# Attention values as seven block products for eight, placed product by product beside FFN chunks 0 and 1

## The chip, the cores and the metric

One core of a Trainium2 chip. The metric is the device time of the kernel in microseconds (us). The engines that matter here are TensorE (PE; PEld is its weight load, which overlaps the matmuls), VectorE (DVE), ScalarE (ACT), GpSimd (POOL) and SyncE (SP, which only issues DMAs). Each engine runs its own list of instructions strictly in order, so an instruction that waits holds up everything listed behind it on the same engine.

## The reference

A gated mix of two branches over the same 2048 tokens of 512 channels, in float32:

```
q, k, v = split(x @ wqkv)                  # 32 heads of 16 channels
idx  = pos - 2 * arange(8)                 # 8 keys per token, two apart; earlier than 0 is masked
o    = einsum(softmax(q . k[idx] / 4), v[idx])
a    = o @ wo
b    = (gelu(x @ w_gate) * (x @ w_up)) @ w_down      # hidden width 1792
g    = sigmoid((x * gate_w).sum(-1))
out  = g * a + (1 - g) * b
```

## The kernel before

**Parities.** Because the keys lie two tokens apart, even and odd tokens never meet. The kernel handles the even tokens (parity 0) and then the odd ones (parity 1), 1024 tokens each, as two blocks of 512. The first block's x, split by channel halves, is called a11 and a12; the second's a21 and a22. Weights are cut the same way into b11, b12, b21 and b22.

**Split operands.** Every float32 operand is kept as a rounded part ("hi", written by ACT) and the rest ("lo", the raw value minus hi, made by DVE, or by ACT and an adding POOL DMA for the FFN weights). A product of 128-deep operands is three matmuls: hi·hi, lo·hi, hi·lo. A block product over 256 channels is therefore six matmuls.

**Seven for eight.** The gate and up projections of the FFN, and the keys and queries, are made by a seven-product scheme for 2x2 blocks: instead of eight products it uses a11·b11, a12·b21, s1·t1, s2·t2, s3·t3, s4·b22 and a22·t4, where s1 to s4 are sums of token blocks and t1 to t4 sums of weight blocks. The values did not use it: `values(par, jj)` (L174) made, for each of the 8 token tiles jj of a parity, two results of 258 and 256 columns, each from four channel chunks times three matmuls (`qkv_mm`, L124), 192 matmuls a parity. The first result carries two extra columns, of which one is the logit z of the mixing gate.

**Stages.** `start()` (L867) makes keys and queries of parity 0 and prepares the operands of what follows. `ffn(0)` runs 14 FFN chunks; `kq_second()` (L1121) does for parity 1 what `start()` did; `ffn(1)` and an output stage follow. `gate_up` (L521) makes one FFN chunk: seven products into PSUM tiles X_, Z_ and W_ of pool "p" (four banks), with ACT copies (`copy`, L464; the copy of X_ to W_, L539) and DVE adds (`add`, L469) between them; the seventh, a22·t4, is put off into the next chunk (`fourth`). Between its products it calls `idle(i, n)`, which runs side jobs set with `at(i, ...)`, and `piece(i)`. In chunks 0 and 1 the pieces are the value tiles, from chunk 2 on they are the down projection.

**FFN operands.** `operands(par, f, i)` (L403) makes chunk f's weight parts: ACT writes minus the raw value's rounding (L416), a POOL DMA adds the raw value (L417), ACT writes hi (L421). The sums t1 to t4 of the raw weights come from DVE (`combine`, L398; for chunks 0 and 1 of parity 0 `sums`, recorded at L787). A group 0 tile (g with 768 columns hi and 768 lo) holds t1, t2 and b11; group 1 holds the other four.

**Attention.** DVE does nearly all of it: multiplies of 128x2048 (L225, L287) and reductions of the same size (L228), 32 of each kind, with smaller adds. `pull(budget)` advances it by about so many us of work at each call. Its first unit reads the tile kq, whose first rows are filled by a shifted copy (`shift`, L148, two DMAs on ACT's queue for the second half of parity 0).

**Order.** A scheduler places the instructions on the engines by its own estimate of times and by priority; attention has a lower priority than the rest. `Row` (L775) keeps the stages in `start()` and `kq_second()` in the order written, and all that goes through `row`, `act` and `mms` shows under one line, L787. `after` and `ordered` add dependencies by hand.

Of the kernel before, what the change touches and what calls it, by code (L numbers as in the profile page):

```python
# [25 lines left out]
WT = KC * WQ  # L26
WA = 576
DW = 1088
VL = 544
UC = 128  # L30
# [18 lines left out]
def tile_gated_mix(ctx: ExitStack, tc: tile.TileContext, xt, wqkv, wff, wo, out):  # L49
# [5 lines left out]

    BUFS = {"A": 6, "S": 8, "g0": 2, "g1": 2, "d": 4, "raw": 2, "hh": 6, "hl": 6, "c": 4, "s": 3,
            "r": 2, "rt": 4, "p": 4, "lg": 2}

    COLS = {"A": 1024, "S": 1024, "g0": 3 * WA, "g1": 8 * QW, "c": WA, "d": DW, "raw": 8 * QW}

# [62 lines left out]

    def qkv_mm(ps, par, jj, cb, kcs, c0=0, cn=512, behind=None):  # L124
        t = slice((jj % BT) * P, (jj % BT + 1) * P)
        for kc in kcs:
            xh, xl = X[par, jj // BT, kc]
            wh, wl = WC[cb, kc]
            for n, (a, w) in enumerate(((xh, wh), (xl, wh), (xh, wl))):
                LAST[:] = [nc.tensor.matmul(ps[:, :cn], a[:, t], w[:, c0:c0 + cn], start=(kc == 0 and n == 0),  # L130
                                            stop=(kc == KC - 1 and n == 2))]
                if behind:
                    ordered(LAST[-1], behind)

    KQ = {}
# [21 lines left out]

    def take(ps, par, jj, hh, tag=None):
        st = tl(tag or next(stages))[:, :512]
        nc.scalar.activation(st[:, :CU], ps[:, :CU], AF.Copy)  # L160
        two = st[:, :CU].rearrange("p (c d) -> p c d", c=2)
        (nc.sync if par else nc.scalar).dma_start(rows(VS[par, hh][:, W:], jj), two)
        if not hh:
            nc.scalar.activation(z[:, par, jj:jj + 1], ps[:, CU:CU + 1], AF.Copy)

    def gates(par, ex=None):
# [6 lines left out]

    def values(par, jj):  # L174
        for hh in range(2):
            ps = bank(f"acc{(2 * jj + hh) % BT}")
            qkv_mm(ps, par, jj, 1, range(KC), (CU, 0)[hh], (WQ, CU)[hh], mms.last if par and jj < 2 else None)
            take(ps, par, jj, hh, tag=None if jj < 5 else "c")
        pull(2.7)
        if jj == NP - 1:  # L180
            done.add((par, 1))

# [301 lines left out]
    def fourth():  # L484
        if late:
            late.pop()()
# [33 lines left out]

    def gate_up(par, f, pieces, do):  # L521

# [15 lines left out]
        W_ = bank("p")  # L538
        nc.scalar.activation(W_, X_, AF.Copy)  # L539
        idle(1, 0.7)  # L540
        piece(0)
# [3 lines left out]
        idle(2, 0.3)  # L545
        fourth()
        product(X_, "s2", w["t2"], False)
        u2 = copy(X_)
        idle(3, 0.7)
# [4 lines left out]
        nc.scalar.activation(c11, W_, AF.Gelu_apprx_tanh)  # L554
        idle(5, 0.7)
        product(Z_, "s4", w["b22"], False)
        c12 = add(Z_, u2)
        idle(6, 0.5)
        piece(2)
        product(X_, "s3", w["t3"], False)  # L560
        c22 = add(X_, p5)
        hidden((f, 0), c11, c12)
        idle(7, 0.7)
        piece(3)
# [9 lines left out]
    def before():  # L574

        room_x(1)
        for k in range(2):
            for i, (n, blk, kc) in enumerate((("a11", 0, 0), ("a12", 0, 2))):
                OP_[n, k], SRC[n, k] = X[1, blk, kc + k], XR[k][:, i * 512:(i + 1) * 512]
        t = tl("g1", F32R)  # L580
        nc.sync.dma_start(t.bitcast(F32), TB)
        name("b11", pairs([t[:, i * 512:i * 512 + 512] for i in range(4)]))
        yield
        hi("a11", 0)
        lo("a11", 0)
        yield
        load_raw("b12", None, 1, 0)
        load_raw("b21", slots("g0", 3, WA) + slots("c", 1), 0, 1)
        yield
        hi("a12", 0)  # L590
        lo("a12", 0)
        yield
        load_raw("b22", None, 1, 1)
        yield
        hi("a11", 1)
        lo("a11", 1)
        yield

    def ffn(par):
        XOP.update(((n, kc), X[par, blk, kc + k]) for n, blk, k in (("a11", 0, 0), ("a12", 0, 2), ("a22", 1, 2))  # L600
                   for kc in range(2))
        todo = iter(())
        for f in range(FC):
# [5 lines left out]
            if f > 1:  # L609
                pieces = [[lambda b=b, i=i: down(par, f // 2 - 1, f % 2 * 2 + i, b)] for b in range(2) for i in range(2)]  # L610
            else:
                pieces = [[lambda jj=jj: values(par, jj) for jj in jjs]
                          for jjs in (((0, 1), (2, 3), (4, 5), ()), ((6, 7), (), (), ()))[f]]
            if f + 1 < FC:
                for i in range(2):
                    steps = operands(par, f + 1, i)
                    at(1 + 2 * i - (not par and f == 1), next, steps, None)
                    at(5 + i - (not par and f == 1), next, steps, None)
                at(0 if f != 1 else 5, fetch_d, f + 1)
                if f == 1:  # L620
# [19 lines left out]
            else:  # L640
# [12 lines left out]
            gate_up(par, f, pieces, do)  # L653
        for _ in todo:
# [212 lines left out]
    def start():  # L867
        room_x(0)
        wr = stage("prod", (2, W, UC))
        b11, b21 = wr[:, :1024], wr[:, 1024:]  # L870
        b12 = stage("v", (2 * NP - 1, UC))[:, :1024]
        b22 = stage("tb", (2, BT * UC))
# [27 lines left out]
        g1b = [t4_[:, i * 512:i * 512 + 512] for i in range(4)]  # L900
        for kc in range(2):
            X[0, 1, kc] = tl("rt", F32R), tl("rt", F32R)
        for n, blk, kc in (("a11", 0, 0), ("a12", 0, 2), ("a21", 1, 0), ("a22", 1, 2)):
            name(n, [X[0, blk, kc + k] for k in range(2)], [q[k][2 * blk + kc // 2] for k in range(2)])
# [57 lines left out]
        tl("g0")  # L962
        name("b22", pairs(slots("g0", 3, WA) + slots("c", 1)), halves(b22))
        t3_ = [tl(n, F32R) for n in "sssc"]
# [59 lines left out]

        both(hi, "a22", "a21")
        both(lo, "a22", "a21")
        for f in range(2):
            fetch(f)
        fetch_d(0)
        for kc in range(KC):  # L1030
            t = tl("d", F32R)
            h, l = WC[1, kc] = t[:, :WQ + CU], t[:, VL:VL + WQ + CU]
            raw = tl("c") if kc < 2 else (b22, b12)[kc - 2]
            nc.sync.dma_start(raw[:, :CU], wqkv[1, 2, :, kc * WQ:kc * WQ + CU])
            nc.sync.dma_start(raw[:, CU:CU + WQ], wqkv[0, 2, :, kc * WQ:(kc + 1) * WQ])
            OP_["v", kc], SRC["v", kc] = (h, l), raw[:, :WQ + CU]
        sub(b21, b21, b11)
# [44 lines left out]
        done.update(((0, 0), (0, 2)))  # L1082

    def load_pairs(n):
# [5 lines left out]
    def ready():  # L1090

        q = Q2["q"] = [[XR[k][:, i * 512:(i + 1) * 512] for i in range(4)] for k in range(2)]
        load_pairs("t2")
        name("t3", pairs(slots("g0", 3, WA) + slots("c", 1)), halves(RAWS["b12"]))
        yield
# [25 lines left out]
    def kq_second():  # L1121
# [5 lines left out]
        U = [bank(f"acc{t}") for t in range(BT)]  # L1127
        for k in range(2):
            X[1, 1, k] = tl("rt", F32R), tl("rt", F32R)
        name("a21", [X[1, 1, k] for k in range(2)], [q[k][2] for k in range(2)])  # L1130

# [21 lines left out]

        def values_raw(*kcs):
            for kc in kcs:
                SRC["v", kc] = raw = tl("c")[:, :WQ + CU]
                nc.sync.dma_start(raw[:, :CU], wqkv[1, 2, :, kc * WQ:kc * WQ + CU])
                nc.sync.dma_start(raw[:, CU:CU + WQ], wqkv[0, 2, :, kc * WQ:(kc + 1) * WQ])

        def values_room(*kcs):  # L1160
            for kc in kcs:
                t = tl("d", F32R)
                WC[1, kc] = OP_["v", kc] = t[:, :WQ + CU], t[:, VL:VL + WQ + CU]
                hi("v", kc)

        for k in range(2):
# [11 lines left out]
        both(lo, "t4")  # L1178
        values_raw(0, 1, 2)
        block(U, "s3", "t3", False, ask=ASK[3])  # L1180
# [6 lines left out]
        for k in range(2):  # L1187
            sub(q[k][1], q[k][1], s12[k])
        both(hi, "s4", "a21")
        both(lo, "s4", "a21")  # L1190
        values_raw(3)
        for f in range(2):
            fetch_sums(f)
        fetch_d(0)
        values_room(0, 1)
        block(U, "a22", "t4", False, ask=ASK[4])
# [7 lines left out]
        block(Z_, "s1", "t1", True, ask=ASK[5])  # L1204
        values_room(2, 3)
        for t in range(BT):
            join(1, BT + t, Z_[t], u3[t])
        for kc in range(KC):
            lo("v", kc)
        next(steps)  # L1210
        block(Z_, "s4", "b22", False, ask=ASK[6])
        for t in range(BT):
            join(1, t, Z_[t], u2[t])
        for _ in steps:
            pass
# [56 lines left out]
```

## Time and profile before

| | us |
|---|---|
| median of 3 runs | 596.99 (596.58 to 598.38) |
| span of the profiled execution | 594.8 |
| median less span | 2.2 |
| PE busy | 590.1 |
| DVE busy | 529.4 |
| ACT busy | 389.9 |
| POOL busy | 89.2 |

The span runs from the first to the last instruction; the time has 2.2 us around it. The values of parity 0 are made between 44.4 and 77.1 us from the span's start, those of parity 1 between 315.2 and 347.6 us. A row of the timeline gives start, length, engine, line, operation, output <- input, shapes and a count; in brackets the idle time before it and what ended that.

### The profile page before, as it was taken

To read this page: it belongs to the slowest core of one execution; us is meant where nothing else is said; L and a number is where in the kernel's file an instruction comes from. 1 tells how busy PE (TensorE), PEld (TensorE's weight loads), DVE (VectorE), ACT (ScalarE), POOL (GpSimd) and SP (SyncE) were. 2 spreads that over 40 slices of the span, in tenths; PEclk is the share of its full clock that TensorE was granted. 3 is DMA by queue.
4 is the path that set the end of the run, shared out by engine and by line. 5 is a ranking of instruction groups with operands and counts; after the bars stand their busy time and mean duration, and the time that the engine had idled before them with its cause. 6 is when DMAs were issued, how large, how long until landed. Compare 5 with 4: busy or idle time off the path is not lost.

```text
span 594.8 us, 8195 instructions
## 1 busy us (share of the span) xinstructions
PE 590.1 (99%) x2778; PEld 494.1 (83%) x2778; DVE 529.4 (89%) x618; ACT 389.9 (66%) x668; POOL 89.2 (15%) x121
## 2 busy tenths in 40 slices
PE   9999999999999999999999999999999999999997
PEld 6889988888888888888889988888888888888886
DVE  5997979899998999799989888999999989799952
ACT  5845556787679767788773375677668666885532
POOL 0501001111111111102035000111111111101300
PEclk9999999999999999999999999999999999999999
DMA  8789897988989898998589948795967796737924
GB/s 316 264 250 244 238 306 217 261 245 200 273 215 300 225 261 230 240 312 304 192 249 306 276 137 264 168 244 145 272 157 226 183 269 157 220 109 193 143 57 155
DMA packets 80449, 134.18 MB, mean 226 GB/s; under 512 B 8092, under 2 KB 46362, under 8 KB 80152
## 3 DMA queue, kind: packets, MB, share of 16 engines
q1 hardware_dynamic: 62890, 97.67, 49.9%
q0 software_dynamic: 12576, 32.97, 28.4%
q10 hardware_dynamic: 4942, 3.01, 1.6%
q8 instruction: 22, 0.36, 0.3%
q14 instruction: 19, 0.16, 0.1%
HBM read 68.30 MB, written 38.86 MB: 180 GB/s over the span
## 4 chain that ended last, share of the span: by engine, by line
PE 99%; DVE 0%; ACT 0%; issue 0%
PE p L459 45%; PE acc L502 13%; PE p L502 13%; PE acc L130 8%; PE acc L787 8%; PE p L720 5%; PE p L787 5%; PE acc L720 2%; PE p L79 1%; DVE r L766 0%; ACT rt L768 0%; DVE zero L73 0%
## 5 line engine op out<-in xcount | busy, mean ns | idle before, releaser
L459 PE MATMUL p<-S,g 128*128 128x512 f32 x672 | 166.5, 389 | 0.0
L459 PEld LDWEIGHTS p<-S,g 128*128 128x128 f32 x672 | 125.7, 188 | 25.8
L459 PE MATMUL p<-A,g 128*128 128x512 f32 x504 | 126.7, 390 | 0.0
L459 PEld LDWEIGHTS p<-A,g 128*128 128x128 f32 x504 | 94.3, 188 | 19.6
L417 POOL DMA_DIRECT2D g<-raw x40 | 34.5, 862 | 280.3 <-ACT g L416 208.8
L228 DVE TENSOR_REDUCE lg<-prod 128x128 f32<-128x2048 f32 x32 | 72.9, 2279 | 0.1
L502 PE MATMUL p<-d,hh 128*128 128x512 f32 x224 | 68.5, 389 | 0.0
L502 PE MATMUL acc<-d,hh 128*128 128x512 f32 x224 | 58.1, 389 | 0.0
L287 DVE TENSOR_TENSOR prod<-kq,lg 128x2048 f32<-128x2048 f32 x24 | 54.7, 2279 | 0.9 <-PE p L459 0.5
L421 ACT ACTIVATE g<-raw 128x1024 fp32r<-128x1024 f32 (+1 forms) x40 | 39.5, 991 | 19.0 <-PE p L459 19.0
L502 PEld LDWEIGHTS acc<-d,hh 128*128 128x128 f32 x224 | 42.0, 188 | 8.7
L502 PEld LDWEIGHTS p<-d,hh 128*128 128x128 f32 x224 | 42.0, 188 | 8.7
L416 ACT ACTIVATE g<-raw 128x1024 fp32r<-128x1024 f32 (+1 forms) x40 | 39.5, 987 | 12.0 <-DVE raw L398 4.6
L469 DVE TENSOR_TENSOR c<-p,s 128x512 f32<-128x512 f32 x56 | 37.8, 682 | 6.8 <-PE p L459 6.0
L464 ACT ACTIVATE s<-p 128x512 f32<-128x512 f32 x56 | 33.2, 594 | 15.0 <-PE p L459 13.5
L476 DVE TENSOR_TENSOR hl<-c,hh 128x512 fp32r<-128x512 f32 x56 | 38.1, 680 | 5.5 <-ACT hh L475 5.5
L502 PE MATMUL p<-d,hl 128*128 128x512 f32 x112 | 42.8, 389 | 0.0
L475 ACT ACTIVATE hh<-c 128x512 fp32r<-128x512 f32 x56 | 35.1, 628 | 10.7 <-DVE c L473 10.6
L473 DVE TENSOR_TENSOR c<-c 128x512 f32<-128x512 f32 x56 | 38.2, 682 | 4.3 <-ACT c L570 4.1
L518 ACT ACTIVATE rt<-p 128x512 f32<-128x512 f32 x48 | 28.2, 595 | 20.1 <-PE p L502 20.1
L291 DVE TENSOR_TENSOR prod<-prod 128x1024 f32<-128x1024 f32 x32 | 39.0, 1218 | 0.2
L130 PE MATMUL acc<-d,A 128*128 128x256 f32 (+1 forms) x288 | 37.9, 281 | 0.0
(183 smaller groups left out, 982.0 us busy)
## 6 DMA issues: line engine op xcount, KB each, us to landing
g<-raw POOLq DMA_DIRECT2D x27, 512.0 KB, 6.6
raw<-wff SPq DMA_DIRECT2D x42, 256.0 KB, 3.7
ws<-g SPq DMA_DIRECT2D x14, 768.0 KB, 6.2
g<-ws SPq DMA_DIRECT2D x14, 768.0 KB, 5.4
r<-wff SPq DMA_DIRECT2D x28, 256.0 KB, 4.8
d<-r POOLq DMA_DIRECT2D x24, 256.0 KB, 6.4
g<-raw POOLq DMA_DIRECT2D x13, 384.0 KB, 6.4
os<-tb SPq DMA_DIRECT2D x64, 64.0 KB, 3.8
```

The costliest lines, as they stand in the source:

```text
L130: LAST[:] = [nc.tensor.matmul(ps[:, :cn], a[:, t], w[:, c0:c0 + cn], start=(kc == 0 and n == 0), stop=(kc == KC - 1 and n == 2))]
L228: nc.vector.tensor_reduce(two_of(lg, jj), prod.rearrange("p j w (h d) -> p (j w) h d", d=DH), axis=AX.X, op=OP.add)
L287: paced(nc.vector.tensor_tensor(prod.rearrange("p j w (h d) -> p (j w) h d", d=DH), spans(v, jj).rearrange("p j w (h d) -> p j w h d", d=D ...
L291: nc.vector.tensor_tensor(prod[:, :, :4], prod[:, :, :4], prod[:, :, 4:], op=OP.add)
L416: nc.scalar.activation(lo, raw, AF.Copy, scale=-1.0)
L421: ins = nc.scalar.activation(hi, raw, AF.Copy)
L459: LAST[:] = [nc.tensor.matmul(ps, w_, a_, start=(start and kc == 0 and n == 0), stop=(kc == 1 and n == 2), skip_group_check=True)]
L473: nc.vector.tensor_tensor(ge, ge, up, op=OP.mult)
L476: nc.vector.tensor_tensor(hl_, ge, hh_.bitcast(F32), op=OP.subtract)
L502: ins = nc.tensor.matmul(pp, a[:, ts], w, start=(i == 0 and n == 0 and gr == 0), stop=(i == 1 and n == 2), skip_group_check=True)
L720: ins = nc.tensor.matmul(pa, a, b, start=(first and n == 0), stop=(last and n == 2), skip_group_check=True)
L787: return lambda *args, **kw: self.add(getattr(self.eng, name)(*args, **kw))
```

## The change

`values` becomes a generator that makes the values by the seven-product scheme. For each of four pairs of tiles (tile t of the first block with tile t of the second) the steps a to g are the products a11·b11, s1·t1, s2·t2, a12·b21, s4·b22, s3·t3 and a22·t4, six matmuls each, into three PSUM banks (X, W, Z). ACT copies X to W after step a. Results leave by ACT (steps b, c, d, g) or by a DVE add (steps e, f). `PLAN` puts the 28 steps of a parity at six places in each of chunks 0 and 1. That is 168 matmuls a parity for 192. The token sums s1 to s4 are those that the FFN uses and were there already; x's block a21, which only the old values needed, is no longer split (four ACT copies and four DVE subtractions fewer in the kernel). The weight blocks need seven split operands for four, and five block subtractions and a small copy for the gate column. `fetch_d` and the buffer sizes are moved accordingly.

```diff
+    STAGES = (("r", "r"), ("hh", "hl"), ("s", "s"), ("s", "s"))
+    def value_steps(par, t):
+        x_, w_, z_ = (f"acc{i}" for i in ((0, 3)[t % 2], 1, 2))
...
+        def prod(ps, a, w, cols, start=False):
+            for k in range(2):
+                ah, al = XOP[a, k]
+                wh, wl = (x[:, k, :cols] for x in VO[w])
+                for n, (x, y) in enumerate(((ah, wh), (al, wh), (ah, wl))):
+                    LAST[:] = [nc.tensor.matmul(ps[:, :cols], x[:, ts], y, start=start and k == 0 and n == 0,
+                                                stop=k == 1 and n == 2, skip_group_check=True)]
...
+        def first(ps, jj, st):
+            put(st[:, :CU], ps[:, :CU])
+            (nc.sync if par else nc.scalar).dma_start(rows(VS[par, 0][:, W:], jj), two(st[:, :CU]))
+            put(z[:, par, jj:jj + 1], ps[:, CU:CU + 1])
+        def second(ps, jj, st):
+            nc.vector.tensor_tensor(st[:, CU:], ps[:, :CU], st[:, CU:], op=OP.add)
+            nc.sync.dma_start(rows(VS[par, 1][:, W:], jj), two(st[:, CU:]))
+        def a():
+            T["x"] = bank(x_)
+            prod(T["x"], "a11", "b11", WQ, True)
+            T["w"] = bank(w_)
+            put(T["w"][:, :WQ], T["x"][:, :WQ])
+        def b():
+            T["z"] = bank(z_)
+            prod(T["z"], "s1", "t1", CU, True)
+            put(staged(1)[:, CU:], T["z"][:, :CU])
+        def c():
+            prod(T["x"], "s2", "t2", WQ)
+            put(staged(0)[:, CU:], T["x"][:, :CU])
+        def d():
+            prod(T["w"], "a12", "b21", WQ)
+            first(T["w"], t, staged(0))
+        def e():
+            prod(T["z"], "s4", "b22", CU)
+            second(T["z"], t, staged(0))
+        def f():
+            prod(T["x"], "s3", "t3", CU)
+            second(T["x"], BT + t, staged(1))
+        def g():
+            prod(T["x"], "a22", "t4", WQ)
+            first(T["x"], BT + t, staged(1))
+    PLAN = (("a0 b0", "c0 d0 a1", "e0 f0 d1", "b1 g0 c1", "e1 f1 a2", "d2 g1 c2 b2"),
+            ("f2 e2 a3", "g2 d3", "b3", "c3 e3", "f3", "g3"))
+    def values(par):
+        steps = [value_steps(par, t) for t in range(BT)]
+        for chunk in PLAN:
+            for place in chunk:
+                for n in place.split():
+                    steps[int(n[1])][n[0]]()
+                    pull(0.77)
...
+                yield
...
+                if f:
+                    at(0 if f != 1 else 5, fetch_d, f + 1)
+                else:
+                    for g_ in range(2):
+                        at(6 + g_, fetch_d, g_)
...
-        both(hi, "a22", "a21")
-        both(lo, "a22", "a21")
+        both(hi, "a22")
+        both(lo, "a22")
...
-        both(hi, "v")
+        value_hi("b11")
         sums(0)
         parts(0)
-        both(lo, "v")
+        value_lo("b11")
+        value_sum("t1")
+        value_hi("t1")
+        value_lo("t1")
         put(BT, U[0])
-        for kc in (2, 3):
-            hi("v", kc)
-            lo("v", kc)
+        value_hi("b21")
+        value_lo("b21")
         put(BT + 1, U[1])
+        value_sum("t2")
+        value_hi("t2")
+        value_lo("t2")
+        value_gate()
         parts(1)
         put(BT + 2, U[2])
         put(BT + 3, U[3])
+        value_sum("t3")
+        value_hi("b22")
+        value_lo("b22")
+        value_hi("t3")
+        value_lo("t3")
+        value_sum("t4")
+        value_hi("t4")
+        value_lo("t4")
         shift(0, act, BT - 1, NP - 1)
         sums(1)
```

In the changed kernel the helper lines move: what was L787 is L901, the FFN products are L564, the value products L216, the value copies L230 and the value adds L238.

Three places in the order of instructions follow. On PE, from the start of chunk 0 of parity 0 (names of FFN products begin with p; acc tiles are the value banks), before:

```order
L459 MATMUL p<-A,g_542 128x512 x2
L130 MATMUL acc_612<-d,A 128x258 x2
L459 MATMUL p<-A,g_542 128x512 x4
L130 MATMUL acc_612<-d,A 128x258 x3
L130 MATMUL acc_629<-d,A 128x256 x5
L459 MATMUL p<-S,g_542 128x512 x6
```

and now (acc_605, acc_612 and acc_617 are X, W and Z of tile 0; acc_659 is X of tile 1):

```order
L564 MATMUL p<-A,g_533 128x512 x6
L564 MATMUL p<-S,g_533 128x512 x12
L216 MATMUL acc_605<-d,A 128x258 x6
L216 MATMUL acc_612<-d,A 128x258 x6
L216 MATMUL acc_605<-d,S 128x258 x6
L564 MATMUL p<-A,g_556 128x512 x2
L564 MATMUL p<-S,g_556 128x512 x4
L216 MATMUL acc_617<-rt,S 128x256 x6
L216 MATMUL acc_659<-d,A 128x258 x6
```

Values no longer fill in inside the first FFN product; three FFN products come first, then the steps a0, d0 and c0 of tile 0 directly behind each other.

On ACT, in the same chunk, the two shift DMAs into kq and the first parts of chunk 1's FFN weights, before:

```order
L539 ACTIVATE p<-p 128x512
L787 DMA kq<-kq 112x512
L787 DMA kq<-kq 15x512
L464 ACTIVATE s<-p 128x512
L416 ACTIVATE g_603<-raw 128x768
```

and now (g_626 is chunk 1's group 0):

```order
L230 ACTIVATE r<-acc_617 128x256
L230 ACTIVATE r<-acc_605 128x256
L230 ACTIVATE r<-acc_612 128x256
L230 ACTIVATE z<-acc_612 128x1
L234 DMA vs_86<-r 128x2x128
L901 ACTIVATE d<-c 128x2x258
L901 DMA kq<-kq 112x512
L901 DMA kq<-kq 15x512
L230 ACTIVATE acc_666<-acc_659 128x258
L662 ACT_TABLE_LOAD
L662 ACTIVATE c<-p 128x512
L521 ACTIVATE g_626<-raw 128x768
```

The shift now stands behind the copies that empty tile 0's banks, and the first write of chunk 1's weights behind the shift and behind the table load for gelu.

Where chunk 0 passes into chunk 1, on DVE the end of the operand work and the first attention multiply (prod<-kq), before:

```order
L787 TENSOR_TENSOR raw<-raw 128x2x256
L787 TENSOR_TENSOR raw<-raw 128x256 x2
L225 TENSOR_TENSOR prod<-kq 128x2048
L228 TENSOR_REDUCE lg<-prod 128x16x8
L225 TENSOR_TENSOR prod<-kq 128x2048
```

and now:

```order
L901 TENSOR_TENSOR raw<-raw 128x2x256
L574 TENSOR_TENSOR c<-p,s 128x512 x2
L901 TENSOR_TENSOR raw<-raw 128x256
L330 TENSOR_TENSOR prod<-kq 128x2048
L238 TENSOR_TENSOR r<-acc_617,r 128x256
L578 TENSOR_TENSOR c<-c 128x512
L238 TENSOR_TENSOR r<-acc_605,r 128x256
L901 TENSOR_TENSOR raw<-raw 128x256
```

and on PE at the same place, now:

```order
L564 MATMUL p<-A,g_626 128x512 x2
L216 MATMUL acc_719<-rt,S 128x256 x6
L216 MATMUL acc_605<-d,A 128x258 x6
L564 MATMUL p<-A,g_626 128x512 x4
L216 MATMUL acc_719<-rt,S 128x256 x6
```

The value adds that empty Z and X of tile 0 (steps e0 and f0) now stand behind the first attention multiply, and on PE the steps b1 (acc_719, the bank that e0 used) and g0 (acc_605) come between the hi-only matmuls of chunk 1's first product and its four others, the first that use the lo parts of g_626.

More of the change, by code (lines that the diff above doesn't have):

```diff
@@ L172, in gates, with wide @@
         nc.vector.tensor_scalar(gc[:, par], g[:, par], -1.0, 1.0, op0=OP.mult, op1=OP.add)
[L174 to L181, printed above, removed]
+    VO, VR = {}, {}
+    def wide(t):
+        return t.rearrange("p (k c) -> p k c", k=2)
@@ new lines, in value_gate, with staged, two, put @@
+    def value_gate():
+        row.tensor_copy(VO["t2", "z"], VO["b11", "z"])
+    STAGES = (("r", "r"), ("hh", "hl"), ("s", "s"), ("s", "s"))
+    def value_steps(par, t):
+        ts = slice(t * P, (t + 1) * P)
+        x_, w_, z_ = (f"acc{i}" for i in ((0, 3)[t % 2], 1, 2))
+        T = {}
+        def prod(ps, a, w, cols, start=False):
[5 more added lines that the diff above has]
+                                                stop=k == 1 and n == 2, skip_group_check=True)]
+                    if par and not t and start:
+                        ordered(LAST[-1], mms.last)
+        def staged(i):
+            if ("s", i) not in T:
+                T["s", i] = tl(STAGES[t][i])[:, :512]
+            return T["s", i]
+        def two(o):
+            return o.rearrange("p (c d) -> p c d", c=2)
+        def put(o, ps):
+            nc.scalar.activation(o, ps, AF.Copy)
+        def first(ps, jj, st):
[29 more added lines that the diff above has]
+            first(T["x"], BT + t, staged(1))
+        return dict(zip("abcdefg", (a, b, c, d, e, f, g)))
@@ L557, in gate_up @@
         c12 = add(Z_, u2)
+        next(extra, None)
         idle(6, 0.5)
```

157 lines of the change are left out of this document (92 added, 65 removed).

## The prediction

> **What bounds the kernel now.** I read the page's busy line first, then the chain of waits, then the busy times of the two stretches in which values are made.
>
> ```profile
> PE 590.1 (99%) x2778; PEld 494.1 (83%) x2778; DVE 529.4 (89%) x618; ACT 389.9 (66%) x668; POOL 89.2 (15%) x121
> ...
> PE 99%; DVE 0%; ACT 0%; issue 0%
> ...
> 55.37 5.69 PE acc L130 x48
> ...
> 88.21 6.80 PE p L459 x30
> ...
> 44.41:77.13 32.72, 32.72 (x236) 30.65 (x235) 28.28 (x26) 18.58 (x46) 2.62 (x3) 1.00 0.85 244
> ...
> 315.17:347.61 32.44, 32.44 (x235) 30.68 (x234) 28.82 (x27) 12.55 (x32) 6.60 (x9) 1.00 0.89 265
> ```
>
> The chain is PE from end to end: whatever PE does not have to do is gained, and whatever it waits is lost, one for one. A busy PE alone would not prove that, since ends of matmuls are modelled; the starts do. 48 value matmuls start in 5.69 us, 0.1185 us each, 30 FFN matmuls in 6.80 us, 0.2267 each, so six of them, one block product, take 0.71 and 1.36 us. In both windows (length, then busy time of PE, PEld, DVE, ACT, POOL, then clock) the clock is full. DVE is the second limit: 28.3 and 28.8 us busy of 32.7 and 32.4.
>
> **What is removed.** 24 value matmuls a parity, 48 in all: 48 x 0.1185 = 5.7 us, 2.85 a parity. This is the whole gain. The rest asks how much PE waits for what the new order makes late.
>
> **What is added on DVE and ACT.** Subtractions, from the rows of before:
>
> ```profile
> 44.22 0.96 DVE L787 TENSOR_TENSOR g<-raw,g 128x768 fp32r<-128x768 f32 x1 [0.46 <-ACT g L787]
> 45.10 1.29 DVE L787 TENSOR_TENSOR d<-c,d 128x514 fp32r<-128x514 f32 x2
> ...
> 47.51 1.22 DVE L787 TENSOR_TENSOR g<-raw,g 128x1024 fp32r<-128x1024 f32 x1
> ...
> 54.32 2.29 DVE L225 TENSOR_TENSOR prod<-kq 128x2048 f32<-128x2048 f32 x1 [4.06 <-DMA kq<-kq]
> ...
> L398 DVE TENSOR_TENSOR raw<-raw 128x256 f32<-128x256 f32 x24 | 9.9, 414 | 0.0
> ```
>
> A 512-column operation holds DVE about 0.60 us (two in 1.2 us up to the next row's start). A parity loses six lo parts (four values, two of a21), 3.6 us, and gains seven lo parts, 4.2, four sums and the copy, 2.6, and eight adds of 256 columns at about 0.34 (414 ns less the overlap), 2.7: 5.9 us more, 11.8 in both. ACT gains one hi part (seven for six) and four 256-column copies a parity, about 1.6 us; at 66% that alone is cover enough. On DVE the cover of parity 0 is the 4.06 us that it idled for kq, plus the delay of attention, which has no user before the end of the run.
>
> **Chunk 0 of parity 0, where the bill falls.** I followed the three lists by these rows.
>
> ```profile
> 44.41 0.63 PE L459 MATMUL p<-A,g 128*128 128x512 f32 x2
> 44.88 0.41 PE L130 MATMUL acc<-d,A 128*128 128x258 f32 x2
> 45.23 1.20 PE L459 MATMUL p<-A,g 128*128 128x512 f32 x4
> ...
> 72.16 0.88 PE L130 MATMUL acc<-d,A 128*128 128x258 f32 x6
> 72.87 0.87 PE L130 MATMUL acc<-d,rt 128*128 128x256 f32 x6
> ...
> 48.13 0.63 ACTq L787 DMA_DIRECT2D kq<-kq  x1
> 48.20 0.66 ACT L539 ACTIVATE p<-p 128x512 f32<-128x512 f32 x1
> 48.80 1.37 ACTq L787 DMA_DIRECT2D kq<-kq  x1
> ...
> 50.71 0.84 ACT L416 ACTIVATE g<-raw 128x768 fp32r<-128x768 f32 x1
> 51.45 0.38 ACT L160 ACTIVATE hh<-acc 128x256 f32<-128x256 f32 x1
> ...
> 62.90 1.28 ACT L554 ACT_TABLE_LOAD   x1 [0.43 <-ACT hl L160]
> ...
> 73.07 0.39 ACT L160 ACTIVATE c<-acc 128x256 f32<-128x256 f32 x1 [0.85 <-PE acc L130]
> ```
>
> (1) The first product's third matmul needs the lo parts that DVE ends at 45.2 (row 44.22 + 0.96). Before, two value matmuls filled in; now nothing does: 0.3 us. (2) Three FFN products end near 48.8 and step a0 near 49.5. Step d0 follows at once, but reads the bank into which ACT copies a0's result. A product's last result reaches ACT 0.2 us after the next group starts (73.07 against 72.87) and the copy takes 0.39; and ACT, held up behind its first copy, which waits for the first product until 46.3, comes to it with about 0.15 us of arrears. So d0 starts near 50.3: 0.75 us. (3) Step c0 needs t2, whose hi part stands behind that copy on ACT and its lo part behind that on DVE: done near 51.5, 0.3 us after PE asks. (4) Steps d1 and f1 follow their bank's copy closely: 0.2. Sum of the small ones 1.55 us.
>
> One rule speaks against this form: the Trainium skill (Perfetto Trace Analysis, Matmuls) wants independent groups to rotate through PSUM banks, so that one is emptied while the next is filled. By that rule each of some 20 reopened banks a parity waits about 0.65 us (0.2 + 0.39 and a little), 26 us in all; it is the last of the rivals below.
>
> (5) The shift into kq goes out behind the copies of b0, c0 and d0 and t4's hi part, near 56 to 58 us, not 48.1. DVE reaches its first multiply near 59, waits for kq and then works 2.2 us, and e0's and f0's adds stand behind it.
>
> ```profile
> kq<-kq ACTq DMA_DIRECT2D x1, 224.0 KB, 4.0
> ...
> kq<-kq ACTq DMA_DIRECT2D x1, 30.0 KB, 5.4
> ...
> 51.85 0.91 POOL L417 DMA_DIRECT2D g<-raw  x1 [25.54 <-ACT hh L160]
> ...
> g<-raw POOLq DMA_DIRECT2D x1, 384.0 KB, 4.7
> ...
> DMA to landing us min/median/max: 4.2/6.5/9.9
> ```
>
> The two landed 4.0 and 5.4 us after their issue. With an issue at 56 to 57, kq is there at 60 to 62.4, the multiply ends at 62.2 to 64.6, and b1, which PE reaches at about 63 (44.4, plus 18.5 us of matmuls), waits 0 to 2 us, g0 0.2 more. (6) Right behind, PE needs the lo parts of g_626: ACT's first write ends near 60.2 (copy 0.3, table load 1.3, gelu 0.5, write 0.75 behind the shift), POOL issues 0.25 us later (51.55 to 51.85 before), and the DMA takes 4.7 by its own row of this stretch, 4.2 to 9.9 over all forty: 65.2, against 64.5 without any wait. (5) and (6) overlap, the later counts: I take 1.25, between 0 (both early) and 7 (issue at 61.9 after a slow shift, landing 9.9).
>
> Parity 0: 1.55 + 1.25 = 2.8 us, less the gain of 2.85: nothing is left. Bounds 1.0 to 8.5.
>
> **Parity 1.** Here chunk 0's group 0 is loaded ready-made, the value steps may start inside the last key product, and PE's list has steps of two tiles between each bank's uses. Walking it the same way I find e0 0.3 us behind b0's copy and t2, and 0.3 of small change: 0.6 us, bounds 0.2 (no more than now) and 2.0 (three waits like d0's). Gain 2.85 - 0.6 = 2.25.
>
> **The later run.** DVE has 11.8 us more to do in a time 2 us shorter. Its idle time takes that, but an FFN add that comes late holds a bank of pool "p": 0.3 us, bounds 0 and 2. At the end, the last attention result has this to spare:
>
> ```profile
> 574.48 0.71 DVE L300 STREAM_TRANSPOSE tb<-o 128x512 f32<-128x512 f32 x1
> ...
> 581.74 0.69 DVE L88 TENSOR_TENSOR hl<-raw,hh 128x512 fp32r<-128x512 f32 x1 [6.55 <-ACT hh L87]
> ...
> 586.33 0.62 PE L720 MATMUL p<-S,hh 128*128 128x512 f32 x2
> ```
>
> DVE ends that operand at 582.4 and PE first reads it at 586.3: 3.9 us. PE comes 2 us earlier, so DVE may end its attention at most 1.9 us later than now.
>
> **Sum.** -5.7 + 2.8 + 0.6 + 0.3 = -2.0 us: a span of 592.8 for 594.8, and with the 2.2 us by which the median of the runs stands over the span, 595.0.
>
> **The rivals.**
>
> *The covers hold.* The shift and the lo parts of g_626 land early, and only the copies cost: parity 0 1.0, the rest 0.5. -5.7 + 1.5 = -4.2: 592.8. For it: the same DMAs took as little as 4.2 us, and ACT has much free time. Against: every row above is a median or the nearest row, not a pessimistic one.
>
> *Slower: the lo parts of g_626 land last.* Their place on ACT is behind two DMA issues (0.63 and 1.37 us before) and a table load, and the DMA share of the first window is already 0.85. If ACT writes at 61.6 and the DMA takes 8.5 us, they land at 70.4 and PE, there at 64.5, waits 5.9: -5.7 + 1.55 + 5.9 + 0.9 = +2.7, 599.7. It decides against the change from a landing at about 69.5. The Trainium skill (TensorE: Matmul & The Clock Gate, HAM oscillation) says that a gap over about 3.4 us drops the clock to half for a window; the two windows show 1.00, no wait of before is that long, and by the rule such a wait would cost some 1.7 us more, an estimate.
>
> *DVE becomes the bound.* If the 11.8 us do not fit into the idle time and attention ends 4 us later than now, the last operand comes 2.1 us after PE asks: -2.0 + 2.1 = 0.1, 597.1. For it: between 520 and 565 DVE hardly idles. Against: nearly all of the added work lies before 350 us, with idle time behind it.
>
> *Every reopened bank waits.* If all 40 steps that reopen a bank wait 0.65 us, PE loses 26 us: 595.0 + 24, about 619. For it: three banks serve seven products. Against: in PE's list only a0 and d0 stand back to back, and before, ACT emptied a bank in 0.4 us while the next group of 0.7 us ran. The Trainium skill's rule on rotating banks, quoted above, is this case.
>
> **Chances.** Forecast 45%, its own range 593.5 to 596.3, so half of it beyond 0.3% (1.8 us, about what a measurement of this kernel can tell from no change; 595.2); covers hold 22%; slower 21%; DVE bound 10%; every bank 2%. Faster 0.22 + 0.22 = 0.44, same 0.23 + 0.08 = 0.31, slower 0.21 + 0.02 + 0.02 = 0.25. The range reaches from 591.6, where the covers hold almost fully, to 600.0, just past the slower case, and leaves out the far end of that and the last.
>
> **What would show it.** Right: 336 value matmuls at 0.12 us; a PE gap near 0.75 us before d0; DVE waiting for kq until 60 to 62; b1 or the third matmul of chunk 1 as PE's longest wait; parity 1 close to gapless; about 541 us of DVE work. Wrong: value matmuls that take longer beside FFN products, several waits of 0.65 us at reopened banks, gaps in the FFN after 100 us, or an output stage that waits for DVE.

## The result, and the profile after

| | before | changed |
|---|---|---|
| median, us | 596.84 (596.58 to 598.38) | 616.80 (614.64 to 617.98) |
| ratio | | 1.0326 [1.0302, 1.0351] |
| span of the profiled execution, us | 594.8 | 616.2 |

The change makes the kernel 3.3% slower; 595.0 had been forecast. The page of the changed kernel, its busy line and its chain of work:

```profile
PE 595.2 (97%) x2730; PEld 490.7 (80%) x2730; DVE 540.6 (88%) x648; ACT 390.6 (63%) x678; POOL 89.2 (14%) x121
...
PEclk9999999997999999999899999999999999999999
...
PE 70%; issue 10%; DMA 8%; ACT 6%; DVE 5%; SPq 0%; POOL 0%; ACTq 0%; POOLq 0%; DVEq 0%
PE p L564 33%; PE acc L607 9%; PE p L607 9%; PE p L834 5%; PE acc L901 4%; PE p L901 4%; PE acc L216 4%; DMA g<-raw 3%; PE acc L834 2%; DMA raw<-xt 2%; DMA tb<-qs 1%; DMA vs<-s 1%; DVE prod L392 1%; DMA raw<-wff 1%; DVE lg L333 1%
```

PE has the 48 matmuls fewer and DVE the 540.6 us that were worked out, yet the chain, which was PE from end to end, now passes through transfers, ACT and DVE, and two slices show a lower clock.

**Where the time went.** PE's delay at a point is the start of a matmul there less the nominal pitches of all matmuls ahead of it on PE (0.2267 us for 512 columns, 0.1185 for 256 to 258). Taken at the first use of an FFN weight tile, and at the last value step of parity 0:

| at the start of | before: at us, delay | changed: at us, delay |
|---|---|---|
| chunk 0, parity 0 | 44.4, 4.2 | 44.5, 4.3 |
| chunk 2 | 88.1, 4.7 | 84.2, 8.7 |
| the last value step of parity 0 | 77.0, 4.6 | 94.8, 10.4 |
| chunk 4's second tile | 125.7, 4.7 | 128.0, 13.4 |
| chunk 5's second tile | 138.4, 4.7 | 150.8, 19.3 |
| chunk 13 | 252.6, 4.7 | 267.2, 22.5 |
| chunk 0, parity 1 | 318.8, 4.7 | 342.8, 29.9 |
| chunk 3, parity 1 | 373.0, 4.9 | 393.7, 31.5 |
| the last tile | 528.5, 4.8 | 551.7, 31.8 |

The delay grows by 27.5 us for 0.6, less 5.7 for the matmuls saved: 21.2 of the 21.4 us between the spans. 6.1 of it lie where the values of parity 0 are made (their last step comes behind the first product of chunk 2) and 1.6 where those of parity 1 are. The other 19.8 lie in stretches whose products the change did not touch.

Here is what stands ahead of and in the first of those stretches, in the timelines, before and then after (start, length, engine, line, operation, in brackets the idle time and what ended it):

```profile
76.21 0.56 DVE L232 TENSOR_TENSOR lg<-lg,mask 1x392 f32<-1x392 f32 x1
77.66 0.43 SPq L201 DMA_DIRECT2D tb<-qs  x1
83.89 2.29 DVE L225 TENSOR_TENSOR prod<-v,tb 128x2048 f32<-128x2048 f32 x1
```

```profile
90.38 0.55 DVE L337 TENSOR_TENSOR lg<-lg,mask 1x392 f32<-1x392 f32 x1
93.58 0.44 SPq L306 DMA_DIRECT2D tb<-qs  x1
102.94 2.29 DVE L330 TENSOR_TENSOR prod<-v,tb 128x2048 f32<-128x2048 f32 x1 [5.07 <-DMA tb<-qs]
109.89 1.66 PE L564 MATMUL p<-A,g 128*128 128x512 f32 x6 [1.88 <-DVE c L574]
110.46 0.64 ACT L580 ACTIVATE hh<-c 128x512 fp32r<-128x512 f32 x1 [8.45 <-DVE c L578]
111.00 0.83 ACT L521 ACTIVATE g<-raw 128x768 fp32r<-128x768 f32 x1
130.60 0.86 POOL L522 DMA_DIRECT2D g<-raw  x1 [1.54 <-DMA ws<-g]
140.58 4.63 PE L564 MATMUL p<-A,g 128*128 128x512 f32 x10 [2.62 <-DMA g<-raw]
```

The scores of the first attention unit (0,0) end 14 us later (the row with the mask). Only behind them may the three loads of unit (0,1) go out, `v` twice and `tb`; the last is issued at 93.6 instead of 77.7. Before, DVE found them there; now its first multiply of unit (0,1) stands still for 5.07 us, and behind it in DVE's list stand FFN adds and weight sums. PE waits 1.88 us for one of these adds, and ACT 8.45 us for another FFN operation of DVE, with the next chunk's weight copies behind it. The chain of the changed kernel goes on from PE's wait through FFN products to POOL's issue of a weight transfer at 130.60 us; PE runs out of weights until that has landed. Ten matmuls then take 4.63 us, twice their 2.27: the clock is at half.

### The profile page after: what moved, and what is told of

It reads as the page before. It is cut to its first block, busy times and chain, and to the rows that moved or that the text cites. A ratio compares the mean times of both kernels' runs of the same rounds, so it can differ in the third digit from the quotient of the medians.

```text
span 616.2 us, 8089 instructions
## 1 busy us (share of the span) xinstructions
PE 595.2 (97%) x2730; PEld 490.7 (80%) x2730; DVE 540.6 (88%) x648; ACT 390.6 (63%) x678; POOL 89.2 (14%) x121
## 4 chain that ended last, share of the span: by engine, by line
PE 70%; issue 10%; DMA 8%; ACT 6%; DVE 5%; SPq 0%; POOL 0%; ACTq 0%; POOLq 0%; DVEq 0%
PE p L564 33%; PE acc L607 9%; PE p L607 9%; PE p L834 5%; PE acc L901 4%; PE p L901 4%; PE acc L216 4%; DMA g<-raw 3%; PE acc L834 2%; DMA raw<-xt 2%; DMA tb<-qs 1%; DMA vs<-s 1%; DVE prod L392 1%; DMA raw<-wff 1%; DVE lg L333 1%
## 5 line engine op out<-in xcount | busy, mean ns | idle before, releaser
L564 PE MATMUL p<-S,g 128*128 128x512 f32 x672 | 169.0, 390 | 2.0 <-ACT s L569 2.0
L564 PEld LDWEIGHTS p<-S,g 128*128 128x128 f32 x672 | 125.1, 188 | 28.7 <-ACT s L569 2.9
L564 PE MATMUL p<-A,g 128*128 128x512 f32 x504 | 130.7, 396 | 7.5 <-DMA g<-raw 4.5
L564 PEld LDWEIGHTS p<-A,g 128*128 128x128 f32 x504 | 94.6, 191 | 29.8 <-DMA g<-raw 5.6
L607 PE MATMUL acc<-d,hh 128*128 128x512 f32 x224 | 61.0, 390 | 0.2
L551 POOL DMA_DIRECT2D d<-r x24 | 20.5, 855 | 152.8 <-ACT d L550 119.3
```

Source lines behind the costliest of these rows:

```text
L564: LAST[:] = [nc.tensor.matmul(ps, w_, a_, start=(start and kc == 0 and n == 0), stop=(kc == 1 and n == 2), skip_group_check=True)]
L607: ins = nc.tensor.matmul(pp, a[:, ts], w, start=(i == 0 and n == 0 and gr == 0), stop=(i == 1 and n == 2), skip_group_check=True)
```

## The experiments

All times are medians against the kernel before on the same chip. Theory A: the loss follows from the late first attention unit and its late loads. Rival B: the added work of DVE and ACT costs it. Rival C: the order that the scheduler makes of the later chunks is bad in itself. Where an expectation counts experiments, the fifth is the one with early keys, the sixth the one with loads behind the second score step in the changed kernel, the eighth the one with c tiles and new values in parity 1 only, the ninth early keys with c tiles, and the twelfth that with the shift issued by POOL.

**Which parity.** Two mixtures of the old value routine and the new: first new values in parity 1 only, then in parity 0 only. The old routine and its operands are put back for the other parity.

```diff
-todo, extra = iter(()), values(par)
+todo, extra = iter(()), values(par) if NEW[par] else iter(())
```

> Parity 0 makes its values in the old way (four d tiles, a21 split again), parity 1 in the new way. Of the 27 us that PE waits more in the changed kernel, some 18 fall between 44 and 267 us of the run (parity 0) and some 9 behind that. Theory A (the late first attention unit of parity 0, whose late loads stop DVE with FFN work behind it): 594 to 598, no wait of 2 us of PE between 85 and 290 us. Rival B (DVE and ACT just have too much work, 5.9 us of it a parity): about half of the loss, 604 to 608. If the 7 us lost about the start of the second key stage are parity 1's own: 600 to 604.

599.31 us, ratio 1.0023 [1.0004, 1.0042], between the ranges set down.

> Parity 0 makes its values in the new way, parity 1 in the old way. Theory A: nearly the whole loss stays, 609 to 617, with DVE's wait of some 5 us for the loads of the second attention unit near 100 us. Rival B: about half, 604 to 608.

616.13 us, 1.0312 [1.0278, 1.0346]. Nearly the whole loss belongs to parity 0; B's even split is out. But parity 1 did not bring its 2 us in the first mixture either, and the trace of that one names a second cause, on ACT and PE:

```profile
350.16 0.36 SPq L269 DMA_DIRECT2D vs<-s  x1
353.84 0.60 ACT L599 ACTIVATE s<-p 128x512 f32<-128x512 f32 x1 [4.40 <-DMA vs<-s]
354.49 2.80 PE L594 MATMUL p<-S,g 128*128 128x512 f32 x6 [2.00 <-ACT s L599]
```

The value results of tile pairs 2 and 3 are staged in pool `s` (the table `STAGES`), out of which the FFN copies its products too. ACT's copy waits until a transfer of values has read the tile. The old routine staged in hh, hl and c.

**Late keys in the old kernel.** The kernel before, its values untouched, with the second half of the shift issued late. Attention is recorded only from there on, and its share of work up to there is made up at once:

```diff
-        shift(0, act, BT - 1, NP - 1)
...
+                if not par and not f:
+                    at(5, shift_late)
```

> The kernel before, but the second half of the shift into kq is issued behind chunk 0's fourth product, as late as the changed kernel issues it, so that the first attention unit starts some 6 us later; the values and all sums of work are as before. Theory A: a good part of the loss without the change, 602 to 612. Rivals B and C: within 2 us of before, 595 to 599.

619.41 us, 1.0342 [1.0289, 1.0395]: as much as the whole loss, without one new instruction, and above the range set down. It starts the first unit at 66.9 us, 12.6 later than before and more than I meant; its scores end at 90.9, as in the change. The same picture stands in its trace:

```profile
106.07 2.29 DVE L225 TENSOR_TENSOR prod<-v,tb 128x2048 f32<-128x2048 f32 x1 [8.75 <-DMA tb<-qs]
109.02 2.93 PE L464 MATMUL p<-A,g 128*128 128x512 f32 x6 [5.12 <-DVE c L474]
```

With the three loads issued earlier, behind the second score step instead of behind the last:

```diff
-                after(ins, SCORED[-1])
+                after(ins, SCORED[-1] if u > 1 else REDUCED[-1])
...
+            if i == 4:
+                load_kq(0, 1)
```

> The kernel before with the late shift (619.41) and with the loads of unit (0,1) issued behind the second score step, as in the run ahead of this. Theory A: DVE's wait of 8.75 us for tb is gone and with it the greater part of the loss: 600 to 608. If the late shift does its harm elsewhere (rival C, the order in which the scheduler then puts the lists): 614 to 620.

603.72 us, 1.0108 [1.0084, 1.0131]. Of 22.0 us, 15.7 went with the wait. What is left is mostly one wait of PE of 3.73 us near 86 us, behind which the clock is at half; there ACT waits 4.84 us for a staging tile.

**Earlier loads in the changed kernel**, called ahead of all scores, and behind the second score step.

> The changed kernel, but the three loads of attention unit (0,1) are called ahead of the scores of unit (0,0) and no longer paced behind them. Theory A: DVE's wait of 5.07 us for tb is gone and with it most of the 13 us that PE loses between 85 and 159 us: 602 to 606. Rivals B (too much work) and C (the list that the scheduler makes of FFN chunks 2 to 13 is at fault, whatever the load): 613 to 618.

610.99 us, 1.0241 [1.0206, 1.0276].

> The changed kernel with the loads of attention unit (0,1) issued behind the second of the four score steps of unit (0,0), between where the change has them and where the run before this one but two had them (ahead of all scores, 610.99). If there the early loads only moved the wait onto the POOL transfer of g near 69 us by sharing the DMA engines with it, this is better than that: 602 to 608. If the late loads are not the cause: 613 to 618.

616.23 us, 1.0326 [1.0293, 1.0359]. Both missed. DVE no longer waits for `tb`, but in the first PE waits 3.29 us near 69 us for a POOL transfer of weights (that the loads beside it make it late is not shown), and in the second ACT waits 3.48 us for an s tile and PE 2.42 us behind it. Early loads alone do not bring the time back.

**Early keys in the changed kernel**: the shift, and the weight sums of chunk 1, ahead of the operands t3, b22 and t4 of the values.

```diff
+        shift(0, act, BT - 1, NP - 1)
+        sums(1)
         value_sum("t3")
...
-        shift(0, act, BT - 1, NP - 1)
-        sums(1)
```

> The changed kernel with the second half of the shift into kq issued right behind the last key copies, and the weight sums of FFN chunk 1 made, ahead of the operands t3, b22 and t4 of the values, not behind them. Theory A (the loss follows from the late first attention unit, whatever makes it late): the first multiply near 55 us for 60.7, the scores end near 84 for 90.4, and half of the loss is gone, 603 to 609. Rival B (too much work on DVE and ACT) and rival C (the new list as such): 613 to 618.

607.81 us, 1.0182 [1.0165, 1.0199], as theory A has it: the scores end at 83.6, and no wait for `tb` is left.

**Other staging tiles**, alone and with the above:

```diff
-    STAGES = (("r", "r"), ("hh", "hl"), ("s", "s"), ("s", "s"))
+    STAGES = (("r", "r"), ("hh", "hl"), ("c", "c"), ("s", "s"))
```

> Old values in parity 0, new ones in parity 1, as in the first experiment (599.31), but the results of the third pair of tiles are staged in tiles of pool c in place of pool s, out of which the FFN copies its products. There ACT waited 4.40 us for an s tile that a transfer of values still read, and PE 2.0 us behind it at a lower clock. If that wait is what eats the gain of parity 1: 594 to 596. If the seven products cost as much elsewhere: 598 to 601.

596.32 us, 0.9993 [0.9983, 1.0003], with new values in parity 1 only.

> The changed kernel with nothing but the third pair of tiles staged in pool c in place of s. If the staging tiles were the main cause of the loss: 603 to 608. If the late attention unit is, and the staging takes some 3 us of the 20 (1.7 near 87 us, 1.3 near 370 us): 612 to 615.

606.08 us, 1.0138 [1.0121, 1.0156]: 10.7 us gone, in the range set down for staging tiles as the main cause and not in that for late attention with 2 to 5 us of staging. Its scores still end at 90.7 and its last load goes out at 93.9. But that load lands after 7.8 us instead of 9.2, and DVE comes to it 2 us later; so DVE waits 1.63 us instead of 5.07, and PE no longer runs out of weights at 140. From chunk 2's second tile to chunk 6 PE's delay grows by 2.6 us instead of 9.4. Why the staging tile changes all this is not shown.

> The fifth experiment (shift into kq and sums of chunk 1 ahead of the operands t3, b22 and t4 of the values, 607.81) with the third pair of tiles staged in pool c as in the eighth, in both parities. There ACT waited 3.0 us near 86 us and longer near 360 us for an s tile that a transfer of values still read; PE lost 2.5 and 5.4 us about it. If the late attention and the staging tiles are the two separate causes: 599 to 602. If the staging only gives room for another wait: 605 to 608.

599.06 us, 1.0033 [1.0021, 1.0046]. Apart, the two edits took off 9.0 and 10.7 us, together 17.7: nearly separate in effect, and nearly the whole loss.

**The work alone**: the kernel before with ten idle subtractions.

```diff
+        for _ in range(10):
+            sub(b11[:, :512], b21[:, :512], b21[:, 512:])
```

> The kernel before with ten more subtractions of 512 columns on DVE (6 us, whose result nobody reads) behind the operands of FFN chunk 0, where the change adds its own; shift, values and transfers as before. Rival B (the added work itself costs this much): 604 to 612, half of the loss or more. Theory A (the work is taken by DVE's idle time as long as the first unit's keys are early): 596 to 600.

601.52 us, 1.0076 [1.0054, 1.0097], between the two. The work costs 4.4 us, by the same path: the scores end at 82.0 for 76.2, and DVE waits 3.46 us for `tb`. Rival B is a part of the loss, not the whole.

**The multiply moved instead of the loads**: the changed kernel, unit (0,1) recorded later.

```diff
         load_kq(0, 1)
+        yield 16.0
         yield from scores(0, 1)
+        yield -16.0
```

> The changed kernel with nothing changed but the place of attention unit (0,1) in DVE's list: its first multiply, which waits 5.07 us for the loads, stands two FFN adds, two hl subtractions and three weight sums further behind. Loads, transfers, staging and amount of work are as in the change. If the harm is done by the FFN work that stands behind the waiting multiply: 606 to 612. If it is done by late attention in itself, or by the s tiles alone: 614 to 619.

617.89 us, 1.0328 [1.0299, 1.0357]. The narrow form of theory A falls. DVE's wait for `tb` is gone (it idles 2.21 us before that multiply, put down to PE), no FFN work stands behind it, and from chunk 2's second tile to chunk 6 PE's delay grows by 1.8 us instead of 9.4. Yet nothing is gained: attention is later still, and PE pays afterwards. From chunk 6 to chunk 13 the delay grows by 7.5 us instead of 2.8, most of it behind a wait of 3.13 us for a weight transfer at 187 us, and through the key stage of parity 1 by 11.5 instead of 7.4. There ACT waits for the kq tile, which the last units of parity 0 still read:

```profile
317.40 0.38 ACT L903 ACTIVATE kq<-p 128x256 f32<-128x256 f32 x1 [6.45 <-DVE prod L392]
320.18 7.17 PE L903 MATMUL acc<-g,A 128*128 128x512 f32 x24 [4.62 <-ACT hh L903]
```

**The shift off ACT.** In the version at 599.06 the issue of the two shift transfers holds ACT, and the copies of the value banks come late behind it (this execution, at 600.70, is 1.6 us above the median):

```profile
52.95 3.43 ACTq L901 DMA_DIRECT2D kq<-kq  x2
56.43 0.63 ACT L901 ACTIVATE rt<-tb 128x512 fp32r<-128x512 f32 x1 [3.24 <-issue]
61.95 0.38 ACT L230 ACTIVATE acc<-acc 128x258 f32<-128x258 f32 x1
62.38 1.07 PE L216 MATMUL acc<-d,A 128*128 128x258 f32 x6 [1.69 <-ACT acc L230]
```

> As the ninth experiment (early shift, sums of chunk 1 early, third pair staged in c; 599.06), with the two transfers of the shift issued by POOL, which is idle there, and not by ACT. In the ninth they held ACT for 3.4 us (52.95 to 56.4), the copies of the values' banks came late behind them, and PE lost 5.1 us between 53 and 67 us, waits of 0.81 and 1.69 us and a lower clock. If that hold is the cause: 594 to 596.5, faster than the kernel before. If the copies are late for their number: 598 to 600.

611.70 us, 1.0229 [1.0197, 1.0260].

> As the twelfth, with the two transfers issued by SP, behind the eight key and query stores that it issues there, in place of POOL. If only ACT's hold matters: within 1 us of the twelfth, 594 to 597. If SP's order makes the keys late again: 598 to 604.

612.37 us, 1.0240 [1.0216, 1.0265]. The POOL run did what was meant in chunk 0, the SP run in part (of 5.1 us by which PE's delay grows there from 53 to 67 us, 0.6 were left with POOL and 3.6 with SP). Both lost far more later. In the POOL run, SP and DVE:

```profile
87.49 0.55 DVE L337 TENSOR_TENSOR lg<-lg,mask 1x392 f32<-1x392 f32 x1
88.07 0.41 SPq L314 DMA_DIRECT2D v<-ks  x1
92.12 1.13 SPq L315 DMA_DIRECT2D v<-ks  x1
93.29 0.92 SPq L306 DMA_DIRECT2D tb<-qs  x1
105.47 2.29 DVE L330 TENSOR_TENSOR prod<-v,tb 128x2048 f32<-128x2048 f32 x1 [11.02 <-DMA tb<-qs]
107.68 0.68 DVE L574 TENSOR_TENSOR c<-p,s 128x512 f32<-128x512 f32 x1
...
111.81 2.93 PE L564 MATMUL p<-A,g 128*128 128x512 f32 x6 [4.64 <-DVE c L574]
```

Here the scores end in time, but on SP's list other transfers stand between the three loads. So they were given a higher priority, and in a last version also issued one score step earlier.

```diff
-        loads = load_slots(k, KS[par, hh][c])
...
+        with tc.high_priority(offset=BEHIND + AHEAD if (par, u) == (0, 1) else 0):
+            loads = load_slots(k, KS[par, hh][c])
...
```

> The twelfth experiment (611.7) with the three loads of attention unit (0,1) in one piece on SP's queue. In the twelfth the second and third stood behind six other transfers and were issued 4 to 5 us after the first; DVE waited 11.02 us for tb, PE 4.64 us behind it and 7 us in all, at a lower clock. If that wait is the whole difference: the loads issued by 89 us, no wait of DVE over 2 us, and 594 to 600. If the list of the twelfth is bad in itself: 608 to 613.

608.72 us (601.58 to 610.86), 1.0148 [1.0101, 1.0195]. By the traces DVE's list is the same as in the POOL run up to and with this multiply, its 114th operation, and so are PE's first 528 matmuls; only SP's order differs up to there:

```profile
85.61 0.42 SPq L316 DMA_DIRECT2D v<-ks  x1
86.07 0.51 SPq L317 DMA_DIRECT2D v<-ks  x1
86.63 0.42 SPq L308 DMA_DIRECT2D tb<-qs  x1
93.65 2.28 DVE L332 TENSOR_TENSOR prod<-v,tb 128x2048 f32<-128x2048 f32 x1
```

No wait, and from chunk 2's second tile to chunk 6 PE's delay grows by 0.5 us instead of 7.0. The profiled execution is the fastest of the six; by the median it is the second range (608 to 613) that came, and what the four at 609 to 611 us lost is not seen.

> As the one ahead of this, with the loads issued behind the third of the four score steps of unit (0,0), some 5 us earlier still, so that they land before the scores end. If DVE's wait for these loads is what decides, whatever else is in the list: 593 to 597. If other waits take its place, as in the sixth experiment: 600 to 612.

599.85 us, 1.0047 [1.0033, 1.0062], between the ranges set down, and steadily, within 1.1 us over ten executions. With the last load issued at 79.5 us DVE waits 1.52 us; no wait over 1.2 us of PE is left. Its interval overlaps that of the version at 599.06 (1.0021 to 1.0046), which keeps the shift on ACT: the two cannot be told apart.

Side by side, by the traces: end of the first unit's scores, issue of the last load, DVE's wait for it, and what PE's delay grew by from chunk 2's second tile to chunk 6.

| run | scores end | last load | wait | growth |
|---|---|---|---|---|
| before | 76.2 | 77.7 | 0 | 0.0 |
| work alone | 82.0 | 84.8 | 3.46 | 2.8 |
| early keys | 83.6 | 85.3 | 0 | 0.8 |
| early keys, c tiles | 86.2 | 87.6 | 0 | 0.5 |
| c tiles alone | 90.7 | 93.9 | 1.63 | 2.6 |
| the change | 90.4 | 93.6 | 5.07 | 9.4 |
| late keys, old values | 90.9 | 93.4 | 8.75 | 10.2 |
| shift by POOL | 87.5 | 93.3 | 11.02 | 7.0 |
| shift by SP | 89.0 | 94.9 | 11.30 | 4.3 |
| shift by POOL, loads with priority | 85.0 | 86.6 | 0 | 0.5 |

The growth goes with the wait, but not in proportion to it.

No version beats the kernel before by more than its measurement can tell; the best is new values in parity 1 alone, staged in c (0.9993 [0.9983, 1.0003]).

## Why the prediction was wrong, point by point

**What was right.** That PE's waits are lost one for one, the 5.7 us, and the added work of DVE: busy for 540.6 us for "about 541". (ACT's busy time grew by 0.7 us, where 1.6 a parity had been put.) The value matmuls run at their old pitch (24 in a row take 2.87 us of the chain, 0.12 each), so the rival in which every reopened bank waits is wrong; that its 619 came out near the time is chance. The output stage does not wait for DVE, so DVE did not become the bound at the end. The sign named for being wrong that did come is "gaps in the FFN after 100 us".

**Chunk 0 of parity 0: right mechanism, sizes low.** The two waits after three FFN products are there, and a smaller one for the lo parts of g_626; further on PE waits for ACT's copy into an s tile, which itself stands still for 2.26 us until DVE is done:

```profile
50.66 0.99 PE L216 MATMUL acc<-d,A 128*128 128x258 f32 x6 [0.61 <-ACT acc L230]
52.10 0.96 PE L216 MATMUL acc<-d,S 128*128 128x258 f32 x6 [0.45 <-ACT g L901]
...
66.02 1.21 PE L564 MATMUL p<-A,g 128*128 128x512 f32 x4 [0.53 <-DMA g<-raw]
...
86.38 0.60 ACT L569 ACTIVATE s<-p 128x512 f32<-128x512 f32 x1 [2.26 <-DVE lg L333]
87.03 1.66 PE L564 MATMUL p<-S,g 128*128 128x512 f32 x6 [1.23 <-ACT s L569]
```

Terms (1) to (3), put at 1.35 us, cost 2.1 (delay 4.3 at 44.5 us, 6.5 at 52.9). Terms (5) and (6) were put at 1.25 and are no more than 0.9: the lo parts of g_626 landed 0.53 us after they were asked for, so the slower rival's landing at 70 us did not occur. Up to the last value step, at 94.8 us, the sum is 6.1 for 2.8, within the bounds of 1.0 to 8.5; 1.4 of it come with the wait for the s tile, which no term had.

**Parity 1**: 1.6 us for 0.6, within 0.2 to 2.0. In the first mixture it is 4.3 (the delay goes from 5.3 to 9.6). What no term had was again the staging tile: the list of waits went through banks and operands and not through pool `s`, which the change shares with the FFN.

**The step that failed** is the cover for DVE's added work and for the late keys: "plus the delay of attention, which has no user before the end of the run", and with it "The later run ... 0.3 us, bounds 0 and 2". The term put at 0.3 measured 19.8 us. The delay has users long before the end. One is SP, which issues the loads of unit (0,1) only behind the scores of unit (0,0); the loads of `tb` took 5.4 to 12.5 us in these runs, and DVE, which runs its list in order, meets them with FFN adds queued behind. The other is the key stage of parity 1, which writes the kq tile that the late units still read. DVE's 65 us of idle time over the run do not help, because they do not lie between those two points and the work that is late. The prediction looked at the end of the run for DVE's slack and never asked what the first unit's end triggers.

The runs show the path, not each share of it: late keys alone are enough for the loss in the old kernel; earlier keys took 9.0 us off the change and other staging tiles 10.7. Why the staging took three times what its own waits show stays open: most of its gain lies in the stretch of the late load, though the scores end no earlier. Every edit also lets the scheduler order the later chunks anew, and only the POOL run and the one with higher priority have the same lists up to the wait; so rival C is not excluded for a part of the loss. Of the 7.4 us lost from chunk 13 to the end of the key stage, the chain of the changed kernel names the late load of x, a transfer of 5.54 us, and DVE's late multiply; PE's longest wait there, 2.30 us at 302.6, is for ACT. No run separated these.

## What to carry to other kernels

For work that is declared free because it is off the critical path, find what its end triggers: here a load that is issued behind it, a tile that comes free behind it, and the in-order list in which the next user of both stands ahead of critical work. An idle share of 11% says nothing of that; the spare time between one such end and its next user does. Count shared buffer pools among the resources of a new stage, with the transfer's landing, not its issue, as the moment of release.

## What the runs showed of the hardware

**The clock can fall after shorter waits than expected.** The granted clock of three stretches (length, busy times, then clock) behind a wait of PE: of 2.62 us in the changed kernel, of 2.00 in the first mixture, of 1.90 in the run with early keys.

```profile
140.00:146.00 6.00, 5.42 (x13) 4.26 (x14) 2.66 (x3) 1.55 (x3) 0.00 (x0) 0.50 0.70 189
```

```profile
354.40:357.20 2.80, 2.71 (x7) 2.14 (x8) 2.73 (x2) 1.62 (x5) 0.00 (x0) 0.55 0.00 0
```

```profile
86.90:89.50 2.60, 2.57 (x10) 1.91 (x11) 2.59 (x5) 2.36 (x6) 0.00 (x0) 1.00 0.98 395
```

The Trainium skill (TensorE: Matmul & The Clock Gate, HAM oscillation) speaks of gaps over about 3.4 us. Here 2.00 us were enough once, and in the version at 599.06 a wait of 1.69 us was followed by a granted clock of 0.59 (from 62.4 to 66.4 us). Yet behind 1.90 us, and behind 2.58 us in the second mixture (143 to 146 us), the clock stayed at 1.00. So the length of the one wait does not decide it alone. In the changed kernel PE's delay grows by 2.9 us at the half clock behind the 2.62 us wait, and by 1.7 behind the wait at 302.6 us.

**The same load can take twice as long.** In the list of transfers (size, us from issue to landing) the same load of `tb`, 512 KB, landed after 5.9 us before, 9.2 in the changed kernel and 12.1 in the POOL run (where weight loads stand ahead of it on SP), and 6.2 once it was issued ahead of those. That pair of runs is the only one whose other lists agree up to there; in the last version, issued earlier still, the load took 10.3 us.

```profile
tb<-qs SPq DMA_DIRECT2D x1, 512.0 KB, 5.9
```

```profile
tb<-qs SPq DMA_DIRECT2D x1, 512.0 KB, 9.2
```

```profile
tb<-qs SPq DMA_DIRECT2D x1, 512.0 KB, 12.1
```

```profile
tb<-qs SPq DMA_DIRECT2D x1, 512.0 KB, 6.2
```
